# Attention scores of a pair's first three units as four 64 by 64 products each, with the masked block written by ScalarE in advance

## The chip, the core and the metric

The program runs on one core of a Trainium2 chip. The core has five engines with queues of their own: TensorE (PE, matrix products, with the loading of its weights listed apart as PEld), VectorE (DVE), ScalarE (ACT), GpSimd (POOL) and SyncE (SP, which issues most transfers). The metric is the time of one execution in microseconds; of several runs the median counts. Lower is better.

## What is computed

Block-causal attention over 4 batches of 8 heads (576 positions, 64 channels per head, blocks of 64), then two mixture-of-experts layers on the 2304 tokens. The change touches the attention alone:

```python
scores = scale * np.matmul(q, k.transpose(0, 1, 3, 2))
pos = np.arange(S)                                   # S = 576
mask = pos[:, None] // 64 >= pos[None, :] // 64      # blocks of 64
scores = np.where(mask, scores, -1000000000.0)
scores = scores - np.max(scores, axis=-1, keepdims=True)
attn = np.exp(scores)
attn = attn / (np.sum(attn, axis=-1, keepdims=True) + 1e-09)
return np.matmul(attn, v)
```

Behind it `_moe_ref` sends each token to one of 8 experts, or past them, and `_moe2_ref` to two of 8.

## The kernel before

Two heads of one batch make a pair, with their channels on partitions 0 to 63 and 64 to 127; there are 16 pairs, n = 0 to 15, four for each batch. A pair has four units of query rows. Unit 0 holds query tiles 0 and 1 (128 rows each), unit 1 tile 2, unit 2 tile 3, and unit 3 the last 64 rows of both heads. Tile t needs the keys up to position 128(t + 1), so it has 128, 256, 384 or 512 columns of scores. In the last 128 of these, the upper 64 rows must not see the last 64 columns: that corner is the masked block.

The loop from line 957 takes one unit in each turn i and staggers the work. Turn i issues the score products of unit i (`scores`), its row maxima (`highest`), a transposition of the next pair's keys or queries on VectorE (`turned`, in a pair's first two turns, line 542), the transposes of unit i - 2 on TensorE and their copies out of PSUM (`tr`), three steps of the products with V of unit i - 4 (`av`), what stands in `mid`, the exponentials of unit i on ScalarE (`soft`), the rest of `av`, and what stands in `fill`. Each engine runs its instructions strictly in the order in which this loop writes them.

PSUM holds two score buffers, `seta` and `setb`, that units use in turn, the sums of `av` and two single banks, 4 and 5. The two banks are handed out in turn to whoever asks (`bank`, line 72): the transposes of `tr`, those of the finished rows (`turned_rows`, line 693), the router products of a batch (`side_logits`, line 712; in `mid` of the second turn of pairs 5, 9 and 13, and again at the end), and the prefix sums of the routing (`prefix`, lines 187 to 191, two for each batch). A bank is free for the next writer when its copy out is done.

Which of ScalarE and VectorE makes such a copy is decided by `evac` (line 501) when the program is written: it keeps a running sum of planned time for both engines, `load`, that `spend` adds to, and gives the copy to the engine whose sum would be lower. The routing steps are not in these sums. A copy on ScalarE is line 508, one on VectorE line 511.

`scores` (line 549) issues for each tile and each head one product with 64 rows of the array and all its 128 columns; the two heads take the two halves of the rows. `highest` (line 568) first adds -1e9 to the masked block on VectorE (line 575), then takes the maxima (line 578) and scales them (line 585).

Of the kernel before, what the change touches and what calls it, by code (L numbers as in the profile page):

```python
# [8 lines left out]
F32 = mybir.dt.float32  # L9
# [4 lines left out]
AF = mybir.ActivationFunctionType  # L14
OP = mybir.AluOpType
# [4 lines left out]
P = 128  # L20
# [27 lines left out]
def moe_kernel(ctx, tc, q, k, v, w_skip, w_gate, w1, w2, w_gate2, w_noise, noise, w1b, w2b, out):  # L48
    nc = tc.nc
    B, H, S, HD = q.shape  # L50
# [292 lines left out]
    def run(steps):  # L343
        for _ in steps:
            pass
# [135 lines left out]
    with ExitStack() as actx:  # L481
        pa = actx.enter_context(tc.tile_pool(name="pa", bufs=1, space=PSUM))
# [3 lines left out]
        ac = actx.enter_context(tc.tile_pool(name="ac", bufs=1))  # L486
# [8 lines left out]
        def spend(engine, ns):  # L495

            load[engine] += ns
            for e in load:
                load[e] = max(load[e], load[engine] - 2000)
# [36 lines left out]
        SCALE = HD ** -0.5  # L536
# [9 lines left out]
        LAST = 3  # L546
        sets = [0]

        def scores(U):


            kt, qt = flat[U.n]
            U.S = pa.tile([P, 2, 512], F32, name="set" + "ab"[sets[0] % 2])
            sets[0] += 1
            rows = [slice(64 * h, 64 * h + 64) for h in range(2)]
            if U.u < LAST:
                for c, t in U.tiles:
                    for h in range(2):
                        nc.tensor.matmul(U.S[:, h, c:c + (t + 1) * P], qt[rows[h], t * P:(t + 1) * P],  # L559
                                         kt[rows[h], 0:(t + 1) * P], start=True, stop=True, skip_group_check=True)  # L560
            else:
                for w in range(2):
                    for h in range(2):
                        c = (w + h) % 2
                        nc.tensor.matmul(U.S[rows[h], c, 0:288], qt[rows[h], 512:576], kt[rows[h], 288 * c:288 * c + 288],  # L565
                                         start=True, stop=True, skip_group_check=True)

        def highest(U):


            U.negm = wk.tile([P, 4], F32, name="negm", bufs=4)
            if U.u < LAST:
                lo = U.S[0:64].rearrange("p h (a c) -> p h a c", c=64)
                lo = lo[:, :, 1:6:4] if U.u == 0 else lo[:, :, 2 * U.u + 3]
                nc.vector.tensor_scalar(lo, lo, -1e9, None, op0=OP.add)
                spend(nc.vector, 150 + 133 * len(U.tiles))
                for i, (c, t) in enumerate(U.tiles):
                    nc.vector.tensor_reduce(U.negm[:, 2 * i:2 * i + 2], U.S[:, :, c:c + (t + 1) * P], axis=AX.X,
                                            op=OP.max, negate=True)
                    spend(nc.vector, 150 + 2.08 * (t + 1) * P)  # L580
            else:
                nc.vector.tensor_reduce(U.negm[:, 0:1], U.S[:, :, 0:288], axis=AX.XY, op=OP.max, negate=True)
                spend(nc.vector, 150 + 1.04 * S)
            n = 2 * len(U.tiles) or 1
            nc.vector.tensor_scalar(U.negm[:, 0:n], U.negm[:, 0:n], SCALE, None, op0=OP.mult)
            spend(nc.vector, 100)
# [276 lines left out]
        units = []  # L863
        for n in range(NS):
            for u in range(NU):
                U = Obj()
# [53 lines left out]
        for n in range(NS):  # L920
            b, hp = divmod(n, 4)
            i = NU * n + NU - 1 + SK2
# [28 lines left out]
        def first_turned(c0, c1):  # L951
            for i in range(2):
                turned(0, i, c0, c1)

        first_turned(0, CUT)
        i = 0
        while i < len(units) + SK2 or any(j >= i for j in (*fill, *mid)):
            if i < len(units):
                U = units[i]
                n, g = U.n, U.u  # L960
                if g == 0 and n % 4 == 0:
                    new_rows(U.b)
                if g == 0 and 0 < n < NS - 2:
                    load_qk(n + 2)
                if g == 0 and 0 < n < NS - 1:
                    load_v(n + 1)
                scores(U)
                if i == 0:
                    first_turned(CUT, S)
                highest(U)  # L970
                if n == 0 and g == 1:
                    load_v(1)
                    load_qk(2)
                g0 = 1 if n == 0 else 0
                if n + 1 < NS and g0 <= g < g0 + 2:
                    turned(n + 1, g - g0)
            if 0 <= i - SK1 < len(units):
                tr(units[i - SK1])
            main = av(units[i - SK2]) if 0 <= i - SK2 < len(units) else iter(())
            for _ in range(3 if units[i - SK2].u < LAST else 2):  # L980
                next(main, None)
            for f, a in mid.get(i, []):
                f(*a)
            if i < len(units):
                soft(U)
            run(main)
            for f, a in fill.get(i, []):
                f(*a)
            i += 1
# [478 lines left out]
    with ExitStack() as cctx:  # L1468
# [14 lines left out]
        h = [hh, cp.tile([P, FC, M], F32R, name="hl")]  # L1483
# [240 lines left out]
```

## Time and profile before

| | us |
|---|---|
| median of 3 runs | 851.49 |
| lowest and highest run | 850.37, 852.3 |
| the profiled execution | 852.99 |
| span of the profiled execution | 851.1 |
| granted clock of TensorE, mean | 0.991 |

| engine | busy us | share of the span |
|---|---|---|
| TensorE | 813.9 | 96% |
| VectorE | 498.8 | 59% |
| ScalarE | 336.6 | 40% |
| GpSimd | 342.9 | 40% |

The page of the profile gives the busy time of each engine over the whole span. Its chain of work that ended last follows the end back to what released each step. For this change the stretch of the attention counts, about the first 236 us; there the chain, the waits and the timeline have to be read by themselves, because the later stages have other limits. Times of rows are in us from the span's start unless marked ns.

### The profile page before, as it was taken

Reading aid. Unit: us, or ns where it says so; the run is one execution under the profiler, and the core shown is the slowest. Engines: PE = TensorE matmul, PEld = TensorE weight load, DVE = VectorE, ACT = ScalarE, POOL = GpSimd, SP = SyncE. Lnnn points to the kernel's source line nnn. Section 1 sums busy time; section 2 is a strip of 40 time slices with the busy share of each in tenths; the row PEclk is TensorE's granted clock in tenths of the full one; section 3 lists DMA queues with packets and bytes.
Section 4 is the critical chain, followed back from the end, with each engine's and each line's share of the span. In section 5 each row is a group of like instructions: output and inputs, shape, how many; then the busy total and the mean of one; then the engine's idle time right before and its main releaser. Section 6 shows DMA issues by size and latency. Waiting matters only on the chain.

```text
span 851.1 us, 16018 instructions
## 1 busy us (share of the span) xinstructions
PE 813.9 (96%) x5916; PEld 711.0 (84%) x5916; DVE 498.8 (59%) x1470; ACT 336.6 (40%) x608; POOL 342.9 (40%) x286
## 2 busy tenths in 40 slices
PE   6999999999999999999999999999999999999994
PEld 3777777777787768777889999989999899999993
DVE  5777978879543544537747466355562655635631
ACT  4676655565422322313417335324252253423410
POOL 1043220120442315433436048365383572833745
PEclk9999999999999999999999999999999999999997
DMA  7777646662028887987728256355464564541314
GB/s 122 164 143 185 141 119 148 88 125 61 18 72 262 300 276 235 289 205 287 229 47 239 86 140 148 78 144 116 136 127 84 141 140 119 117 77 13 43 16 45
DMA packets 157063, 117.56 MB, mean 138 GB/s; under 512 B 109688, under 2 KB 123760, under 8 KB 156976
## 3 DMA queue, kind: packets, MB, share of 16 engines
q1 hardware_dynamic: 133696, 92.00, 39.5%
q0 software_dynamic: 20848, 24.15, 16.4%
q8 instruction: 48, 0.79, 0.4%
q10 hardware_dynamic: 2432, 0.30, 0.2%
q14 instruction: 39, 0.32, 0.2%
HBM read 95.89 MB, written 22.82 MB: 139 GB/s over the span
## 4 chain that ended last, share of the span: by engine, by line
PE 82%; DVE 6%; DMA 6%; issue 1%; another core or an unknown queue 1%; ACT 1%; SPq 1%; POOL 0%; POOLq 0%; DVEq 0%; ACTq 0%
PE bank L414 23%; PE sums L641 7%; PE bank L1198 5%; PE bank L613 4%; PE bank L1521 4%; PE bank L1523 4%; PE bank L1522 4%; PE bank L457 4%; PE bank L459 4%; PE bank L458 4%; PE seta L559 3%; PE bank L398 2%; PE setb L565 2%; DMA st<-in_moe_w_dram 2%; PE sums L659 2%
## 5 line engine op out<-in xcount | busy, mean ns | idle before, releaser
L1531 POOL DMA_INDIRECT out_dram<-y,toq x77 | 150.4, 1954 | 94.2 <-DVE y L1530 75.0
L414 PE MATMUL bank<-xh,w1h 128*128 128x296 f32 (+2 forms) x512 | 122.0, 299 | 0.8 <-ACT xh L401 0.8
L414 PE MATMUL bank<-xl,w1h 128*128 128x296 f32 (+2 forms) x512 | 120.8, 297 | 0.6 <-DVE xl L402 0.4
L414 PE MATMUL bank<-xh,w1l 128*128 128x296 f32 (+2 forms) x512 | 120.6, 297 | 0.0
L417 ACT ACTIVATE hh<-bank 128x296 fp32r<-128x296 f32 (+2 forms) x128 | 47.5, 412 | 147.7 <-PE bank L414 144.6
L418 DVE SCALAR_TENSOR_TENSOR hl<-bank,hh 128x296 fp32r<-128x296 f32 (+2 forms) x128 | 54.0, 458 | 77.9 <-ACT hh L417 72.5
L414 PEld LDWEIGHTS bank<-xh,w1h 128*128 128x128 f32 x512 | 87.1, 189 | 1.7 <-ACT xh L401 0.9
L414 PEld LDWEIGHTS bank<-xl,w1h 128*128 128x128 f32 x512 | 86.9, 189 | 1.1 <-DVE xl L402 1.1
L414 PEld LDWEIGHTS bank<-xh,w1l 128*128 128x128 f32 x512 | 86.4, 188 | 0.0
L155 ACT ACTIVATE q2h<-st 128x1024 fp32r<-128x1024 f32 x28 | 57.7, 2062 | 61.4 <-PE bank L459 61.4
L641 PE MATMUL sums<-v,ptS 128*128 128x65 f32 x640 | 80.1, 271 | 0.3 <-issue 0.2
L641 PEld LDWEIGHTS sums<-v,ptS 128*128 128x128 f32 x640 | 77.0, 192 | 1.3 <-issue 0.9
L1521 PE MATMUL bank<-hh,q2h 128*128 128x336 f32 x224 | 72.7, 325 | 0.0
L1523 PE MATMUL bank<-hh,q2l 128*128 128x336 f32 x224 | 71.1, 318 | 0.0
L1522 PE MATMUL bank<-hl,q2h 128*128 128x336 f32 x224 | 71.0, 317 | 0.0
L214 POOL DMA_INDIRECT rows<-xd,t3x x35 | 36.2, 1035 | 83.8 <-PE bank L398 76.4
L508 ACT ACTIVATE ptS<-bank 128x384 f32<-128x384 f32 (+2 forms) x97 | 48.1, 524 | 52.0 <-PE bank L613 44.3
L206 POOL DMA_INDIRECT lists<-ent,seats x26 | 25.6, 986 | 104.3 <-DVE seats L844 100.2
L164 DVE TENSOR_TENSOR q2l<-st,q2h 128x1024 fp32r<-128x1024 f32 x28 | 56.3, 2012 | 14.4 <-ACT q2h L155 14.4
L613 PEld LDWEIGHTS bank<-idf,P 128*128 128x128 f32 x320 | 35.0, 144 | 31.3 <-ACT P L595 11.4
L457 PE MATMUL bank<-q2h,hh 128*128 128x512 f32 x136 | 53.8, 396 | 0.0
L458 PE MATMUL bank<-q2l,hh 128*128 128x512 f32 x136 | 53.5, 394 | 0.0
(389 smaller groups left out, 1656.3 us busy)
## 6 DMA issues: line engine op xcount, KB each, us to landing
st<-in_moe_w_dram SPq DMA_DIRECT2D x98, 512.0 KB
r<-in_moe_w_dram SPq DMA_DIRECT2D x32, 512.0 KB
out_dram<-zero SPq DMA_DIRECT2D x19, 256.0 KB
kraw<-in_k_dram SPq DMA_DIRECT2D x60, 72.0 KB
qraw<-in_q_dram SPq DMA_DIRECT2D x60, 72.0 KB
v<-in_v_dram SPq DMA_DIRECT2D x32, 128.0 KB
xd<-Xe SPq DMA_DIRECT2D x2, 1040.0 KB
out_dram<-y,toq POOLq DMA_INDIRECT x77
```

The source lines that it names most:

```text
L155: nc.scalar.activation(h, src, AF.Copy)
L164: on_low.tensor_sub(l, src, h.bitcast(F32))
L414: nc.tensor.matmul(s[i][:, :c1 - c0], a, part[:, c, c0:c1], start=st, stop=sp)
L418: nc.vector.scalar_tensor_tensor(b, r, 0.0, a.bitcast(F32), op0=OP.max, op1=OP.subtract)
L457: nc.tensor.matmul(o[:n], a, wh, start=f == 0, stop=False)
L458: nc.tensor.matmul(o[:n], a, wl, start=False, stop=False)
L613: nc.tensor.transpose(pt[:, c:c + P], U.P[:, h, c:c + P], idf)
L641: nc.tensor.matmul(o[:, h, t, :], U.T[h][:, c + j * P:c + (j + 1) * P], vb[:, j, h, :], start=j == 0, stop=j == t)
L1521: nc.tensor.matmul(o[:, :n], wh, a, start=f == 0, stop=False)
L1522: nc.tensor.matmul(o[:, :n], wh, b, start=False, stop=False)
L1523: nc.tensor.matmul(o[:, :n], wl, a, start=False, stop=f == FC - 1)
L1531: st = nc.gpsimd.indirect_dma_start(out=out.rearrange("n (a d) -> (n a) d", d=P), in_=y, in_offset=None, compute_op=OP.add, out_offset=bas ...
```

## The change

Four things change. The two products of a tile become four: each head's is cut into the upper and lower 64 query rows, g = 0 and 1, that take the left and the right half of the array's columns; the upper half computes 64 columns less, so the masked block is not computed. A new function, `masked_set`, allocates the score buffer two units ahead and lets ScalarE write the constant into the masked block, one copy of 64 x 128 elements for each tile; it stands right behind the exponentials of the unit that used the buffer before. The addition of line 575 goes. And the planned times follow: 300 ns more for ScalarE for each written block, and 283 ns (one tile) or 416 ns (two) less for VectorE for each unit.

```diff
+        hidden = ac.tile([64, 1], F32, name="hidden")
+        nc.vector.memset(hidden, -1e9 / SCALE)
+        masked = []
+
+        def masked_set(U):
+            S = pa.tile([P, 2, 512], F32, name="set" + "ab"[sets[0] % 2])
+            sets[0] += 1
+            if U.u < LAST:
+                for c, t in U.tiles:
+                    lo = S[0:64, :, c + t * P + 64:c + t * P + P]
+                    nc.scalar.activation(lo, hidden[:, :, None].to_broadcast([64, 2, 64]), AF.Copy)
+                    spend(nc.scalar, 300)
+            return S
+
         def scores(U):
             kt, qt = flat[U.n]
-            U.S = pa.tile([P, 2, 512], F32, name="set" + "ab"[sets[0] % 2])
-            sets[0] += 1
+            U.S = masked.pop(0)
             rows = [slice(64 * h, 64 * h + 64) for h in range(2)]
             if U.u < LAST:
                 for c, t in U.tiles:
-                    for h in range(2):
-                        nc.tensor.matmul(U.S[:, h, c:c + (t + 1) * P], qt[rows[h], t * P:(t + 1) * P],
-                                         kt[rows[h], 0:(t + 1) * P], start=True, stop=True, skip_group_check=True)
+                    for g in range(2):
+                        n = t * P + 64 * (g + 1)
+                        for h in range(2):
+                            nc.tensor.matmul(U.S[rows[g], h, c:c + n], qt[rows[h], t * P + 64 * g:t * P + 64 * g + 64],
+                                             kt[rows[h], 0:n], start=True, stop=True, skip_group_check=True)
...
             if U.u < LAST:
-                lo = U.S[0:64].rearrange("p h (a c) -> p h a c", c=64)
-                lo = lo[:, :, 1:6:4] if U.u == 0 else lo[:, :, 2 * U.u + 3]
-                nc.vector.tensor_scalar(lo, lo, -1e9, None, op0=OP.add)
-                spend(nc.vector, 150 + 133 * len(U.tiles))
...
+        masked.extend(masked_set(U) for U in units[:2])
         first_turned(0, CUT)
...
             if i < len(units):
                 soft(U)
+            if i + 2 < len(units):
+                masked.append(masked_set(units[i + 2]))
             run(main)
```

The planner's sums thereby give 48 of its 156 copies to another engine: 34 that were ScalarE's become VectorE's (18 of 128x384 elements, 11 of 128x512), 14 the other way (9 of 64x128). Two places show what that does to the order. Names with numbers are single buffers; `ptS` is the copy of a unit's transposes, `ptS2` its short last piece, `negm` the maxima.

The first place is the second turn of pair 9, on VectorE, from the transposition of the keys on, before:

```order
L542 STREAM_TRANSPOSE kt_1814<-kraw_1610 128x576
L575 TENSOR_SCALAR setb_1854<-setb_1854 64x2x64
L578 TENSOR_REDUCE negm_1857<-setb_1854 128x2
L585 TENSOR_SCALAR negm_1857<-negm_1857 128x2
L542 STREAM_TRANSPOSE qt_1815<-qraw_1611 128x576
L511 COPY ptS2_1870<-bank5_1869 64x128
```

and now:

```order
L542 STREAM_TRANSPOSE kt_1904<-kraw_1689 128x576
L591 TENSOR_REDUCE negm_1950<-setb_1863 128x2
L598 TENSOR_SCALAR negm_1950<-negm_1950 128x2
L542 STREAM_TRANSPOSE qt_1905<-qraw_1690 128x576
L511 COPY ptS_1955<-bank4_1954 128x512
```

The addition is gone, and the copy of the wide transposes out of bank 4 is now the last of these, in the place of the short one out of bank 5. On TensorE the router products take bank 4 right behind it, before:

```order
L559 MATMUL setb_1854<-kt_1633,qt_1634 128x384 x2
L621 MATMUL bank4_1862<-idf_73,P3_1775 128x128 x4
L625 MATMUL bank5_1869<-idf_73,P3_1775 64x128
L641 MATMUL sums_330<-v2_154,ptS_1760 128x65 x3
L712 MATMUL bank4_1876<-xt0_1246,wcat_95 32x128 x4
```

and now (line 712 is line 725 there):

```order
L576 MATMUL setb_1863<-kt_1714,qt_1715 64x320 x2
L576 MATMUL setb_1863<-kt_1714,qt_1715 64x384 x2
L634 MATMUL bank4_1954<-idf_73,P3_1861 128x128 x4
L638 MATMUL bank5_1961<-idf_73,P3_1861 64x128
L654 MATMUL sums_348<-v2_154,ptS_1846 128x65 x3
L725 MATMUL bank4_1968<-xt0_1309,wcat_95 32x128 x4
```

The two score products became four; the order behind them is the same, so the router products now follow a bank that VectorE empties. Pairs 5 and 13 read alike at this place.

The second place is the third turn of pair 10, on VectorE, before:

```order
L542 STREAM_TRANSPOSE qt_2061<-qraw_1792 128x576
L818 TENSOR_TENSOR OH_2146<-e8_80,atb_2099 128x80
L820 TENSOR_TENSOR ohb_2147<-OH_2146 128x40
L821 COPY ent2_2148<-tokc_97 128x10
L575 TENSOR_SCALAR seta_2152<-seta_2152 64x2x64
L578 TENSOR_REDUCE negm_2155<-seta_2152 128x2
L585 TENSOR_SCALAR negm_2155<-negm_2155 128x2
L511 COPY ptS_2166<-bank5_2165 128x384
```

and now:

```order
L542 STREAM_TRANSPOSE qt_2160<-qraw_1880 128x576
L511 COPY ptS2_2234<-bank5_2233 64x128
L831 TENSOR_TENSOR OH_2248<-e8_80,atb_2200 128x80
L833 TENSOR_TENSOR ohb_2249<-OH_2248 128x40
L834 COPY ent2_2250<-tokc_97 128x10
L591 TENSOR_REDUCE negm_2258<-seta_2191 128x2
L598 TENSOR_SCALAR negm_2258<-negm_2258 128x2
L511 COPY ptS_2262<-bank4_2261 128x384
```

VectorE's copy behind the maxima was that of bank 5 and is now that of bank 4. Bank 4 is the one that the second prefix sum (line 187) of that batch takes next, before as now.

## Rows read from the trace of the kernel before

**Rows 1.** Page, first part: busy time, share of the span, instructions.
```profile
PE 813.9 (96%) x5916; PEld 711.0 (84%) x5916; DVE 498.8 (59%) x1470; ACT 336.6 (40%) x608; POOL 342.9 (40%) x286
```

**Rows 2.** Stretches: length, busy us (instructions) of PE, PEld, DVE, ACT, POOL; clock, DMA.
```profile
15.00:65.00 50.00, 50.00 (x428) 38.77 (x424) 38.70 (x88) 34.22 (x68) 11.20 (x16) 1.00 0.81 151
65.00:155.00 90.00, 86.09 (x795) 66.10 (x793) 75.03 (x287) 53.42 (x115) 19.20 (x24) 0.99 0.63 144
```

**Rows 3.** Chain of work, pair 2: start, us, engine, output, line, instructions.
```profile
29.69 0.86 PE seta L559 x8
...
33.24 0.85 PE setb L559 x4
...
36.07 1.06 PE seta L559 x4
37.13 0.81 PE bank L613 x6
37.94 1.73 PE sums L641 x16
39.67 1.12 PE setb L565 x8
...
42.47 0.86 PE seta L559 x8
```

**Rows 4.** Lines 559 and 565: weight loads, ns min/median/max, starts, shapes.
```profile
L559 PEld LDWEIGHTS seta<-kt,qt x192: 182/186/330, 5.3 to 218.6; 64*128 64x128 f32 x192
...
L565 PEld LDWEIGHTS setb<-kt,qt x128: 129/133/228, 14.6 to 224.1; 64*64 64x64 f32 x128
```

**Rows 5.** Timeline, second turn of pair 9: start, us, engine, line, operation [idle before].
```profile
128.47 0.92 PE L559 MATMUL setb<-kt,qt 64*128 64x384 f32 x4
...
129.51 0.29 DVE L575 TENSOR_SCALAR setb<-setb 64x128 f32<-64x128 f32 x1 [1.06 <-PE setb L559]
...
129.83 0.96 DVE L578 TENSOR_REDUCE negm<-setb 128x2 f32<-128x768 f32 x1
...
130.07 0.60 ACT L508 ACTIVATE ptS<-bank 128x512 f32<-128x512 f32 x1 [0.21 <-PE bank L621]
130.72 1.08 PE L712 MATMUL bank<-xt,wcat 128*32 128x128 f32 x32
...
131.70 0.24 DVE L511 COPY ptS<-bank 64x128 f32<-64x128 f32 x1
```

**Rows 6.** Groups of the attention by shape: count, busy us, mean ns, idle before.
```profile
L575 DVE TENSOR_SCALAR seta<-seta 64x256 f32<-64x256 f32 x16 | 6.7, 421 | 1.1 <-PE seta L559 0.8
...
L508 ACT ACTIVATE ptS<-bank 64x128 f32<-64x128 f32 x6 | 1.6, 262 | 3.1 <-PE seta L559 3.1
...
L511 DVE COPY ptS<-bank 128x512 f32<-128x512 f32 x1 | 0.7, 683 | 0.0
```

**Rows 7.** Waits of TensorE from 15 to 225: total us, times, longest.
```profile
PE bank L613 <- DVE ptS L511: 3.4, 3, 1.4
...
PE bank L712 <- ACT ptS L508: 0.6, 1, 0.6
```

**Rows 8.** Timeline, up to the third turn of pair 10.
```profile
143.44 0.42 DVE L575 TENSOR_SCALAR seta<-seta 64x256 f32<-64x256 f32 x1
...
150.73 0.18 PE L187 MATMUL bank<-ohb,tri 128*128 128x40 bf16 x1 [1.00 <-DVE seta L575]
...
150.76 1.22 DVE L578 TENSOR_REDUCE negm<-seta 128x2 f32<-128x1024 f32 x1
...
152.10 0.55 DVE L511 COPY ptS<-bank 128x384 f32<-128x384 f32 x1
```

**Rows 9.** The 3.3 us behind it: a stretch as in Rows 2, and its chain.
```profile
152.60:155.90 3.30, 3.30 (x22) 1.95 (x20) 3.16 (x19) 1.78 (x4) 0.00 (x0) 0.50 0.48 78
...
152.19 1.74 PE setb L565 x8
153.93 1.47 PE bank L613 x6
```

## The prediction

> **What bounds the kernel now.** I read the page's busy shares first, then stretches, then the chain of waits inside the attention. TensorE is busy 96% of the span, no other engine over 59% [rows 1]. The stretches show the same where the change sits: from 15 to 65 us TensorE has no idle time, VectorE is busy 38.7 of the 50 us and ScalarE 34.2; from 65 to 155, where the routing of finished batches is mixed in, TensorE is idle 3.9 of 90 us [rows 2]. The chain of pair 2 says it step by step: from 29.69 to 42.47 all is TensorE, 12.78 us for a pair [rows 3]. So in the attention an edit is worth what it does to TensorE's own products and waits; what it takes from VectorE is worth something only at the places where TensorE waits for VectorE. The later stages begin when the attention ends, and TensorE bounds most of them, so I let a shift of the attention's end come through in full.
>
> The profiled execution took 852.99 us, 1.5 above the median of the runs, 851.49. I make the sum as a difference and add it to either.
>
> **The score products.** What one unit takes: 512 columns 1.06 us, 384 columns 0.85 us [rows 3]. 128 columns more cost 0.21 us, so 512 columns cost 0.84 and some 0.21 us is a fixed part at the unit's start. For 384 columns it is the same: 0.63 + 0.22. The last unit already has products of 64 by 64: 1.12 us for 8 instructions of 288 columns [rows 3]. Two heads run side by side, so four follow one another: 4 x 288 x 1.64 ns = 0.94 (at 2 cycles a column, 0.96), and the fixed part is 0.16 to 0.18. That fits the weight loads: 186 ns with 128 columns of the array, 133 ns with 64 [rows 4]; the difference, 53 ns, is the 0.05 us.
>
> If the two halves of the array's columns run side by side as the two halves of its rows do now, a tile still takes the time of its longer half, which has as many columns as before. The masked block saves no time then; only the shorter weight load is saved, 0.05 us a unit. For unit 0 there is a second effect: it now stands behind products of a quarter of the array and changes the form of product. Within one form no gap shows at all: 16 products with V take 1.73 us, 0.108 each [rows 3]. So of its 0.21 us I take another 0.10 (bounds 0 and 0.16) away, since four-quarter products would follow four-quarter products. A pair: 3 x 0.05 + 0.10 = 0.25 us (bounds 0.10 and 0.31). Eleven of the 16 pairs are bound by TensorE throughout; the first, where TensorE waits for loads, gives 0.1, and four are treated below with their waits. **Minus 2.7 - 0.1 = minus 2.8 us** (bounds minus 1.2 and minus 3.5).
>
> That quarters with the same rows can run together is the one thing that this rests on. The row that bears on it: 32 router products of 128 columns take 1.08 us [rows 5]. They have the same 128 rows and differ in their 32 columns of the array. By the slope above each takes 0.21 us alone over two instructions, 0.105 for one; one after another 32 would take 3.4 us. 1.08 us is eight groups of four and a load. So column parts over one set of rows do run side by side.
>
> The Trainium skill, "TensorE: Matmul & The Clock Gate", Part 3 under "What overlaps and what doesn't", says otherwise of the loading: a weight load overlaps products in flight only when its row group differs, and the halves g = 0 and g = 1 have the same row group. By that rule the two halves would follow one another, which is rival D below. The row of the router products speaks against the rule.
>
> **The additions that go.** 48 of them. The wide one (unit 0) is 0.42 us [rows 6], the others 0.29 [rows 5]: 16 x (0.42 + 0.29 + 0.29) = 16 us of VectorE. In the stretches where VectorE is not the last to be waited for this is nothing. And the planner gives most of it back: VectorE gains 34 copies and loses 14, net 15 of 128x384 at 0.55 us [rows 8], 11 of 128x512 at 0.68 [rows 6], less nine and two short ones that it hands over and four that it takes, some 14 us.
>
> **The mask writes.** 64 blocks, two for unit 0 (4 tiles a pair). The trace has no such write; the nearest row is ScalarE's copy of 64x128 out of PSUM, 262 ns [rows 6]. It reads one value for a block, so I take 0.26 us as its price, with 0.1 to 0.4 as bounds: 17 us of ScalarE (6 to 26), while it loses copies of about 12 us or more. It stands right behind ScalarE's own exponentials of the unit that had the buffer, the next products into that buffer come a turn later, behind transposes, and ScalarE is busy 68% in the stretch [rows 2]. So I cost it at nothing. If that cover is gone, 0.26 us for a unit is at stake (rival E). Queued behind a write on ScalarE are the copies of the next transposes; they come after a turn's products, so a delay of 0.26 us has room.
>
> **The copies that change engine, at the places where TensorE waits.** Here the change adds waits.
>
> Pair 9, second turn: the router products need bank 4. Before, ScalarE copies the wide transposes out at 130.07 in 0.60 us, and the products start at 130.72, right behind it [rows 5]. Now VectorE does this, behind its maxima, their scaling and the transposition of the queries. Maxima at once when the scores are there (129.51 less 0.05, the addition being gone): 0.96 for the maxima [rows 5], 0.12 for the scaling (from the end of the maxima at 151.98 to the copy at 152.10 [rows 8]), 0.78 for the transposition [rows 8], 0.68 for the copy [rows 6]. Together 2.54, and 0.06 for the signals: 132.06 in place of 130.72. **Plus 1.34 us.** The order is the same in pairs 5 and 13. In pair 13 I take the same, **plus 1.34**. In pair 5 TensorE waited 0.6 us at this step already [rows 7], so **plus 0.75**. Bounds for each: 0, if VectorE should come to the transposition early and the products with V behind these steps were to stretch, and 1.6, if VectorE is still in the routing.
>
> Pair 10, third turn: the prefix sum starts at 150.73, having waited 1.00 us for VectorE [rows 8]. Now bank 4 is emptied by VectorE behind the maxima of that turn. These began at 150.76. Three additions ahead of them in a stretch in which VectorE does not pause go (0.42 [rows 8], and two of 0.29), a short copy of 0.24 [rows 5] comes: start at 150.00. From the start of the maxima to the copy are 1.34 us, and the copy takes 0.55 [rows 8]: the bank is free at 151.89, **1.15 us later**. Part comes back behind it, since VectorE comes to the next steps with less queued; I take 0.4 of it, which leaves **plus 0.75** (bounds 0 and 1.15).
>
> In pairs 6 and 14 TensorE waits for VectorE's copies of transposes (three waits, 3.4 us in all, the longest 1.4 [rows 7]). There a copy is 512 wide now and was 64 wide, while an addition of 0.29 goes: 0.68 - 0.24 - 0.29 = 0.15; I take plus 0.1 for each, **plus 0.2**, and no saving of products in these pairs. In pair 15, the third of these waits, the addition goes and nothing comes: **minus 0.3**.
>
> **The sum:** -2.8 + 1.34 + 1.34 + 0.75 + 0.75 + 0.2 - 0.3 = **+1.3 us**: 854.3 for the profiled execution, 852.8 against the median. What is gained 0.05 to 0.1 us at a time is lost at four waits.
>
> **The clock.** From 152.6 to 155.9, behind the wait of pair 10, the granted clock is 0.50, that is 1.2 GHz, and the last unit's products take 1.74 us for 1.12, the transposes 1.47 for 0.81 [rows 3, 9]: 0.62 + 0.66 = 1.3 us for such a stretch. Before it TensorE had stood idle. The new waits make TensorE idle for 1.3 us at places where it did not idle before; whether the clock falls there the trace of before cannot say.
>
> **The rivals.**
> A, the forecast, +1.3 us: 852.8 (851 to 854.3).
> B, faster. The waits are mostly covered (VectorE reaches the copies sooner, because the additions before them are gone as well, or TensorE would have waited later anyway) and the saving stands. Saving at 0.28 a pair, waits of 0.5 to 1 us in all: -3.2 + 0.7 = -2.5, 849; at the bounds 848. For it: no waiting of TensorE from 15 to 65 us; against it: the copy stands behind the maxima in VectorE's order, and an order does not become shorter than its 2.55 us.
> C, slower, by the clock. One to three of the new idle places are followed by a stretch at 1.2 GHz, 1.3 us each: +2.6 to +5.2, so 854 to 856.5. It decides from one such stretch on. For it: the stretch of [rows 9]; against it: the mean clock from 65 to 155 is 0.99 with several waits in it [rows 2].
> D, the four products do not do what is meant: the halves follow one another. Each tile's upper half has 64, 192, 320, 448 columns, 1024 a pair, at 1.64 ns 1.7 us; 16 pairs, 27 us: 879. Against it the router products [rows 5].
> E, a mask write comes late on ScalarE and the next scores wait: 0.26 us for every second unit beyond the first, some 24 places over half the pairs, less cover: +2 us on the forecast, 855.
>
> **How the numbers follow.** A 0.46, B 0.24, C 0.24, D 0.04, E 0.02. A measurement of this kernel can tell about 0.2% from no change, 1.7 us: faster is below 849.8, slower above 853.2. A's middle lies inside, its upper end beyond: 0.36 same, 0.10 slower. B: 0.20 faster, 0.04 same. C, D and E: slower, 0.30. Together faster 0.20, same 0.40, slower 0.40. Since cases of both signs hold much of the chance, the range goes from B's middle to C's end, 848.5 to 856.5, and leaves out D and half of B's better end; A's own range is 851 to 854.3.
>
> **What would show it.** In the profile after: three score units a pair at about 1.01, 0.80 and 0.70 to 0.76 us (D: 1.8 for the 512-column unit); weight loads of 64x64 at 133 ns; the regular pair at 12.5 us in place of 12.78; waits of TensorE at the router products of pairs 5, 9 and 13 for VectorE's copy, 1.3 us each; the prefix sum of pair 10 waiting about 2 us; VectorE's busy time little changed. Wrong if the regular pair stays at 12.8 (then the fixed part is not the weight load), if the router products follow the transposes without waiting, or if stretches at half clock are many.

## The result

The changed kernel is slower: 862.24 us in the median (859.77 to 863.11, four runs) against 851.25 us of before, a ratio of 1.0109 with an interval of 1.0077 to 1.0140. The prediction had 852.8 us with a range up to 856.5. Four of twelve later executions of one kernel of the experiments, the kernel before with three copies, lie over 1.5% above its fastest and are left out of its numbers as slow ones.

| | before | after |
|---|---|---|
| median, us | 851.25 | 862.24 |
| the profiled execution: time, span, us | 852.99, 851.1 | 859.77, 857.9 |
| its mean granted clock | 0.991 | 0.985 |
| granted clock of the other three runs | | 0.983 |

The profiled execution of after is its fastest. I split each time in two: a stretch at 1.2 GHz in which TensorE is busy takes twice as long, so span x (1 - mean clock) is about what the lower clock costs, and span x mean clock is what is left. This is an estimate; the last 10 us of every kernel stand at 1.2 GHz and add the same 5 us or so to each. Before, its profiled execution: 7.7 us by the clock and 843.4 left; after, mean of four runs: 14.2 and 845.8. So **of the 8.9 us between these two some 2.4 are lost at full clock, and 6.5 by the clock.** The medians are 11 us apart, since the profiled execution of before (852.99 us) took longer than any of its runs.

The page of after, first part, answers to [rows 1]:

```profile
PE 814.2 (95%) x6172; PEld 708.2 (83%) x6172; DVE 495.1 (58%) x1443; ACT 343.7 (40%) x652; POOL 342.5 (40%) x286
```

VectorE has 3.7 us less to do, ScalarE 7.1 more: the planner has given the relief back, as forecast. The chain of work of after from 41 to 55 us (start, us, engine, output, line), and two rows of TensorE's timeline that bound a pair, answer to [rows 3]:

```profile
42.11 0.65 PE seta L576 x10
...
45.46 0.81 PE setb L576 x8
...
48.25 1.02 PE seta L576 x8
...
51.81 1.12 PE setb L582 x8
```
```profile
41.80 0.33 PE L576 MATMUL seta<-kt,qt 64*64 64x64 f32 x2
...
54.30 0.33 PE L576 MATMUL seta<-kt,qt 64*64 64x64 f32 x2
```

The unit with 512 columns takes 1.02 us for 1.06, the one with 384 columns 0.81 for 0.85, and unit 0 starts among the last products of the unit ahead. A pair takes 54.30 - 41.80 = 12.50 us in place of 12.78. The saving is 0.28 us where 0.25 was forecast.

Its waits of TensorE from 15 to 235 us (total, times, longest), to be held against [rows 7]:

```profile
PE bank L626 <- DVE ptS L511: 5.9, 5, 2.6
PE bank L725 <- DVE ptS L511: 4.2, 3, 1.4
PE bank L187 <- DVE ptS L511: 1.9, 2, 1.2
```

The three waits at the router products are there, 1.38 to 1.39 us each. The timeline of the second turn of pair 9 (start, us, engine, line, operation, idle before) answers to [rows 5]; behind it TensorE's timeline goes on, and the last fence has two stretches as in [rows 2], the one behind this wait, and one in pair 15:

```profile
128.79 0.96 DVE L591 TENSOR_REDUCE negm<-setb 128x2 f32<-128x768 f32 x1 [1.27 <-PE setb L576]
...
129.79 0.17 DVE L598 TENSOR_SCALAR negm<-negm 128x2 f32<-128x2 f32 x1
...
129.97 0.78 DVE L542 STREAM_TRANSPOSE qt<-qraw 128x576 f32<-128x576 f32 x1
130.67 0.65 DVE L511 COPY ptS<-bank 128x512 f32<-128x512 f32 x1
...
131.38 1.08 PE L725 MATMUL bank<-xt,wcat 128*32 128x128 f32 x32 [1.39 <-DVE ptS L511]
```
```profile
135.52 1.99 PE L576 MATMUL seta<-kt,qt 64*64 64x448 f32 x8
...
138.76 2.27 PE L654 MATMUL sums<-v,ptS 128*128 128x65 f32 x16
```
```profile
15.00:65.00 50.00, 50.00 (x496) 37.82 (x494) 38.48 (x84) 36.79 (x80) 11.14 (x16) 1.00 0.78 152
65.00:155.00 90.00, 82.62 (x854) 62.43 (x851) 70.75 (x257) 53.57 (x128) 19.16 (x24) 0.96 0.62 141
132.70:139.50 6.80, 6.80 (x32) 4.96 (x32) 3.52 (x22) 2.37 (x7) 0.00 (x0) 0.50 0.75 171
228.20:235.20 7.00, 7.00 (x35) 5.21 (x33) 3.46 (x10) 2.12 (x4) 1.73 (x2) 0.51 0.04 3
```

The wait is as long as the prediction said, to 0.05 us. What it did not have is the 6.8 us at 1.2 GHz (0.50) right behind: there the unit with 512 columns takes 1.99 us instead of 1.09.

Where the time comes from is seen in the starts of the score units, after less before. They are 1.18 us ahead when pair 5 begins. Pair 5's router products cost 0.75. From the second to the last unit of pair 9 they fall back by 4.48 us: 1.38 the wait, 3.1 the half clock. Pair 10 costs 0.85 net of a half-clock stretch that before has there too, pair 13 1.32, pair 15 2.70. The last unit starts 7.98 us late (231.58 for 223.60). What is left of these sums, -2.1 us, is the products' saving less smaller waits, such as those for the routing steps on VectorE (1.3 us in three places, 0.7 in before).

Pair 10 (timeline of after, answers to [rows 8]):

```profile
152.94 0.24 DVE L511 COPY ptS<-bank 64x128 f32<-64x128 f32 x1
...
153.24 0.55 PE L626 MATMUL bank<-idf,P 128*128 128x128 f32 x3 [0.72 <-DVE ptS L511]
...
154.98 0.55 DVE L511 COPY ptS<-bank 128x384 f32<-128x384 f32 x1
...
155.59 0.18 PE L187 MATMUL bank<-ohb,tri 128*128 128x40 bf16 x1 [1.18 <-DVE ptS L511]
```

There are two waits. The short copy of bank 5, which I had only counted as 0.24 us in VectorE's order, is itself waited for: the transposes of the second head need that bank, and the copy stands behind the transposition of the queries. And in pair 15 (timeline of after):

```profile
225.68 0.96 DVE L591 TENSOR_REDUCE negm<-setb 128x2 f32<-128x768 f32 x1 [4.75 <-PE seta L576]
...
227.49 0.88 PE L626 MATMUL bank<-idf,P 128*128 128x128 f32 x6 [2.62 <-DVE ptS L511]
```

TensorE waits 2.62 us where before it waited 1.4, the longest of [rows 7], and from 228.2 on it stands at 1.2 GHz; the 2.70 us of pair 15 are both together.

### The profile page after: what moved, and what is told of

The parts are those of the page before. It is cut to its first block, busy times and chain, and to the rows that moved or that the text cites. A ratio compares the mean times of both kernels' runs of the same rounds, so it can differ in the third digit from the quotient of the medians.

```text
span 857.9 us, 16496 instructions
## 1 busy us (share of the span) xinstructions
PE 814.2 (95%) x6172; PEld 708.2 (83%) x6172; DVE 495.1 (58%) x1443; ACT 343.7 (40%) x652; POOL 342.5 (40%) x286
## 4 chain that ended last, share of the span: by engine, by line
PE 79%; DVE 8%; DMA 7%; issue 2%; SPq 1%; POOL 1%; ACT 1%; POOLq 0%; DVEq 0%; ACTq 0%
PE bank L414 23%; PE sums L654 7%; PE bank L1537 4%; PE bank L1539 4%; PE bank L1538 4%; PE bank L1214 4%; PE bank L626 4%; PE bank L457 3%; PE bank L458 3%; PE bank L459 3%; PE seta L576 3%; PE setb L582 2%; PE bank L398 2%; DMA st<-in_moe_w_dram 2%; PE bank L1228 2%
## 5 line engine op out<-in xcount | busy, mean ns | idle before, releaser
L654 PE MATMUL sums<-v,ptS 128*128 128x65 f32 x640 | 82.9, 277 | 0.5 <-DVE Xo L683 0.2
L654 PEld LDWEIGHTS sums<-v,ptS 128*128 128x128 f32 x640 | 79.9, 198 | 1.6 <-issue 0.9
L164 DVE TENSOR_TENSOR q2l<-st,q2h 128x1024 fp32r<-128x1024 f32 x28 | 56.4, 2014 | 14.2 <-ACT q2h L155 14.2
L626 PE MATMUL bank<-idf,P 128*128 128x128 f32 x320 | 49.1, 292 | 7.5 <-DVE ptS L511 5.9
L508 ACT ACTIVATE ptS<-bank 128x512 f32<-128x512 f32 (+2 forms) x76 | 36.7, 499 | 47.1 <-PE bank L626 42.9
```

The costliest lines, as they stand in the source:

```text
L164: on_low.tensor_sub(l, src, h.bitcast(F32))
L626: nc.tensor.transpose(pt[:, c:c + P], U.P[:, h, c:c + P], idf)
L654: nc.tensor.matmul(o[:, h, t, :], U.T[h][:, c + j * P:c + (j + 1) * P], vb[:, j, h, :], start=j == 0, stop=j == t)
```

## The experiments

**Theory 1**: the loss comes from the copies that moved to VectorE. TensorE waits for them, and standing idle brings the clock down behind some of these waits. **Rival 2**: the clock falls by the new products themselves, that use all four quarters of the array, or the mask writes cost time; the moved copies cost only their waits. Medians of before differ between the groups of runs (848.9 to 857.6 us), so each kernel is held against before of its own group. "Clock" is span x (1 - mean clock), "rest" is span x mean clock, means over the runs; for before itself "clock" is 7.6 to 11.0 us, from group to group.

| kernel | median us | ratio to before (interval) | clock us | rest us |
|---|---|---|---|---|
| before, first group | 856.58 | | 10.9 | 844.0 |
| changed, old copies | 852.62 | 0.9959 (0.9929 to 0.9990) | 8.3 | 842.1 |
| changed, three copies back | 856.17 | 0.9988 (0.9956 to 1.0020) | 9.0 | 845.3 |
| before, new copies | 877.05 | 1.0247 (1.0183 to 1.0311) | 24.7 | 850.7 |
| before, three copies | 870.37 | 1.0174 (1.0105 to 1.0243) | 19.8 | 848.1 |
| before, second group | 857.58 | | 11.0 | 844.7 |
| products alone | 855.41 | 0.9967 (0.9935 to 0.9998) | 12.6 | 841.4 |
| changed, waits filled | 860.09 | 1.0023 (0.9995 to 1.0052) | 11.4 | 846.7 |
| before, one copy | 862.04 | 1.0073 (1.0038 to 1.0108) | 13.7 | 847.9 |
| changed | 861.86 | 1.0038 (1.0011 to 1.0065) | 11.7 | 847.4 |
| before, third group | 852.57 | | 8.8 | 842.2 |
| before, three copies, filled | 855.98 | 1.0047 (1.0025 to 1.0069) | 8.0 | 846.8 |
| before, three copies | 860.94 | 1.0095 (1.0058 to 1.0133) | 14.2 | 845.1 |
| changed, old copies | 852.62 | 1.0003 (0.9983 to 1.0023) | 11.1 | 839.6 |
| products alone | 853.76 | 1.0013 (0.9993 to 1.0032) | 10.2 | 841.7 |
| before, fourth group | 853.37 | | 8.9 | 841.9 |
| changed | 859.81 | 1.0088 (1.0056 to 1.0119) | 13.1 | 845.8 |
| changed | 861.38 | 1.0104 (1.0076 to 1.0132) | 13.2 | 846.3 |
| changed, waits filled | 859.45 | 1.0087 (1.0057 to 1.0117) | 13.6 | 844.5 |
| changed, waits filled | 859.46 | 1.0082 (1.0050 to 1.0115) | 12.6 | 844.6 |
| before, fifth group | 848.88 | | 7.6 | 839.3 |
| changed, pair 10's copies back | 848.58 | 1.0008 (0.9989 to 1.0028) | 6.9 | 840.7 |
| changed, pair 10's and the three back | 846.62 | 0.9972 (0.9955 to 0.9989) | 7.3 | 837.5 |

### The copies, all and three

In all kernels that fix the copies, `evac` reads the engine of each of the 156 copies from a string instead of asking the planner:

```diff
-            if load[nc.scalar] + a <= load[nc.vector] + v:
+            made[0] += 1
+            if COPIES[made[0]] == "A":
```

The changed kernel with the string of before:

> The changed kernel with every copy out of the two banks on the engine that it had before the change; only the assignment of the 156 copies is undone. Theory 1 (the loss comes from the copies that moved to VectorE: TensorE waits for them, and behind some of these waits it runs at 1.2 GHz): no wait at the router products of pairs 9 and 13, no stretch at 1.2 GHz behind pair 9, the regular pair stays at 12.5 us, and the time is 3 to 4.5 us below before, about 847.5. Rival 2 (products on all four quarters of the array themselves bring the clock down, or the mask writes cost time): stretches at 1.2 GHz are as long as in the changed kernel, and the time stays above before, 853 to 857.

The changed kernel with its own string, but "A" for the wide transposes ahead of the router products of pairs 5, 9 and 13 (numbers from 1):

```diff
-COPIES[43], COPIES[84], COPIES[121] = "D", "D", "D"
+COPIES[43], COPIES[84], COPIES[121] = "A", "A", "A"
```

> The changed kernel with three of its copies given back to ScalarE: those of the wide transposes out of bank 4 ahead of the router products in the second turn of pairs 5, 9 and 13. Theory 1: the waits there go (0.75 + 1.38 + 1.32 = 3.4 us) and with them the stretch at 1.2 GHz from 132 to 140 us (some 3 us): 855 to 856; the wait of pair 10 and that of pair 15 stay with what follows them. Rival 2 (the clock falls by the products): only the waits go, the stretch stays: 858.5 to 859.

The kernel before with the changed kernel's string, and with its own string but those three "D":

```diff
-COPIES[43], COPIES[84], COPIES[121] = "A", "A", "A"
+COPIES[43], COPIES[84], COPIES[121] = "D", "D", "D"
```

> The kernel before with every copy out of the two banks on the engine that it has in the changed kernel; the products and the additions on VectorE are as before. Theory 1: the waits at the router products of pairs 5, 9 and 13 come, each 0.3 us longer than in the changed kernel since the addition is still ahead of the maxima, and stretches at 1.2 GHz with them: 860 to 865. Rival 2: the waits alone, 4 to 6 us, with no more half clock than before: 855 to 857.

> The kernel before with three copies given to VectorE, those of the wide transposes ahead of the router products in pairs 5, 9 and 13; nothing else. Theory 1: three waits of about 1.0, 1.65 and 1.65 us, and a stretch at 1.2 GHz behind pair 9 of some 3 us: 857 to 859. Rival 2: the waits alone: 855 to 856, with the granted clock at full level from 130 to 150 us.

Measured: the old copies give a kernel 0.4% below before, and its trace has no stretch at 1.2 GHz in the attention. The waits of theory 1 came as expected, but their price is far above it: the three copies alone, without any of the new products, make the kernel before 13.8 us slower, where theory 1 had 6 to 8 and the waits themselves are 4.5 (5.1 for the 0.6 of before). All copies make it 20 us slower. Of the 13.8, 8.9 are clock. The waits of before with three copies from 15 to 235 us, and the 10 us behind the waits of pairs 9 and 13 in the same trace:

```profile
PE bank L716 <- DVE ptS L515: 5.1, 3, 1.7
...
PE bank L187 <- DVE seta L579: 1.0, 1, 1.0
```
```profile
133.88:143.88 10.00, 10.00 (x89) 7.20 (x91) 5.25 (x31) 3.82 (x10) 0.00 (x0) 0.83 0.75 155
194.31:204.31 10.00, 10.00 (x100) 7.63 (x100) 5.84 (x29) 3.27 (x9) 0.00 (x0) 0.83 0.43 107
```

A clock of 0.83 over 10 us is 3.4 us at 1.2 GHz in each. Rival 2 falls as the main cause: the old products lose as much, or more, when they wait. A small share of the new products in the clock is not excluded: alone, further down, they lose 1.6 and 1.4 us more by it than before does, and the changed kernel with old copies 2.6 less in this group but 2.3 more in the third.

### One copy, the products alone, and the waits filled

The kernel before with one "D", for the wide transposes ahead of the router products of pair 9:

```diff
-COPIES[84] = "A"
+COPIES[84] = "D"
```

> The kernel before with a single copy given to VectorE, that of the wide transposes ahead of the router products in pair 9. By theory 1 one wait of 1.7 us (1.38 and the addition of 0.33) and a stretch at 1.2 GHz behind it that costs some 3 us: 4 to 6 us above before. By rival 2 the wait alone: 1.5 to 2 us above before.

Measured: +4.5 us in the median. TensorE's timeline at the place, and the stretch behind it:

```profile
133.14 1.71 PE L716 MATMUL bank<-xt,wcat 128*32 128x128 f32 x32 [1.71 <-DVE ptS L515]
```
```profile
133.40:147.00 13.60, 13.60 (x81) 10.08 (x71) 4.83 (x29) 3.62 (x9) 0.00 (x0) 0.50 0.56 115
```

One wait of 1.71 us is followed by 13.6 us at 1.2 GHz in this execution, which costs 6.8; over ten runs the clock costs 2.7 us more than in before. So a price for a wait, if there is one, exists only as a mean over executions.

The products alone, in the kernel before, with masked block, additions and copies as they were:

```diff
-                    for h in range(2):
-                        nc.tensor.matmul(U.S[:, h, c:c + (t + 1) * P], qt[rows[h], t * P:(t + 1) * P],
-                                         kt[rows[h], 0:(t + 1) * P], start=True, stop=True, skip_group_check=True)
+                    for g in range(2):
+                        for h in range(2):
+                            nc.tensor.matmul(U.S[rows[g], h, c:c + (t + 1) * P],
+                                             qt[rows[h], t * P + 64 * g:t * P + 64 * g + 64],
+                                             kt[rows[h], 0:(t + 1) * P], start=True, stop=True, skip_group_check=True)
```

> The kernel before with one part of the change: four products of 64 by 64 parts for a tile, all of them over the tile's full columns. The masked block is computed, the additions on VectorE stay, and every copy stays on its engine. If the saving comes from the shorter weight load and from unit 0 staying with one form of product, a pair takes 12.5 us as in the changed kernel, and the time is 3 to 4.5 us below before. If it comes from the masked block that is not computed, a pair stays at 12.78 us and the time at that of before.

TensorE's timeline of the products alone:

```profile
41.28 0.33 PE L564 MATMUL seta<-kt,qt 64*64 64x128 f32 x2
...
47.66 1.09 PE L564 MATMUL seta<-kt,qt 64*64 64x512 f32 x8
...
53.78 0.33 PE L564 MATMUL seta<-kt,qt 64*64 64x128 f32 x2
```

A pair takes 53.78 - 41.28 = 12.50 us, as in the changed kernel. So the masked block that is not computed saves TensorE nothing; the products' form does all of it. The whole kernel gains 3.3 us of rest, and 0.3% of time in this group.

Now the changed kernel with useless products in its three waits. They go into columns of the next unit's buffer that its own products overwrite:

```diff
             for f, a in mid.get(i, []):
+                if f is side_logits and i < len(units):
+                    kt, qt = flat[U.n]
+                    for _ in range(2):
+                        for h in range(2):
+                            r = slice(64 * h, 64 * h + 64)
+                            nc.tensor.matmul(masked[0][:, h, 0:384], qt[r, 0:P], kt[r, 0:384], start=True, stop=True,
+                                             skip_group_check=True)
                 f(*a)
```

> The changed kernel with idle work in the place of its three waits at the router products (second turn of pairs 5, 9, 13): four score products of 384 columns, about 1.3 us, are issued right ahead of the router products into columns of the next unit's score buffer that its own products then overwrite. Nothing that counts is computed less or earlier. Theory 1 (TensorE standing idle lets the clock fall): the three waits shrink to 0 to 0.3 us, the products take their place, so the waits give nothing back, but the stretch at 1.2 GHz behind pair 9 goes: 2 to 6 us below the changed kernel on the same chip. Rival 2 (the clock falls by what the products draw): no gain or a loss of up to 1 us, and the stretch stays or grows.

> The changed kernel once more, so that it and the other three have runs on one chip: 9 to 12 us above before, with waits of 1.38 us at the router products of pairs 5, 9 and 13 and one or more stretches at 1.2 GHz between 130 and 160 us.

Filled and unfilled differ by 1.8 us in the median, and only 0.3 us of the means is clock. And the changed kernel itself is here only 0.4% above before: before loses more to its clock on this chip (11.0 us) than where the case was first measured (7.7), the changed kernel less (11.7 for 14.2). Inconclusive, so the same filling went into the kernel before with three copies, where the waits and the loss are larger (480 columns, about 1.9 us, a buffer taken for it):

> The kernel before with three copies given to VectorE (the waits of 1.71 us at the router products of pairs 5, 9 and 13), and idle work in the place of these waits: four score products of 480 columns, about 1.8 us, right ahead of the router products, into columns of the next unit's score buffer that its own products overwrite. Theory 1 (standing idle at these places lets the clock fall behind them): no stretch at 1.2 GHz within 10 us behind the three places, and though TensorE has the same 5 us less for useful work, the time is 5 us or more below that of the same kernel without the filling. Rival 2 (standing idle has nothing to do with it): the same time as without the filling or up to 1 us more, with as much time at 1.2 GHz.

> The kernel before with three copies given to VectorE, once more, beside the filled one on the same chip: 9 to 14 us above before, of which the waits are 4.3 us, the rest stretches at 1.2 GHz.

TensorE's timeline of the filled kernel in pair 9, and its two stretches from 65 to 225 us:

```profile
132.11 1.88 PE L993 MATMUL seta<-kt,qt 64*128 64x480 f32 x8
133.93 1.08 PE L716 MATMUL bank<-xt,wcat 128*32 128x128 f32 x32
```
```profile
65.00:155.00 90.00, 86.68 (x798) 65.81 (x797) 73.53 (x272) 51.32 (x110) 19.22 (x24) 1.00 0.61 140
155.00:225.00 70.00, 66.97 (x600) 50.03 (x599) 55.92 (x205) 39.21 (x87) 15.65 (x16) 1.00 0.41 82
```

The wait is gone, the router products start at 133.93, within 0.1 us of where they start unfilled in the first group's trace (133.88) and in this group's (133.92), as they do in pairs 5 and 13 of this group, and the kernel is **5.0 us faster for doing useless work** (855.98 for 860.94; by the means 4.6, give or take 3.5; theory 1 asked for 5 or more, so this is at its edge). All of it is clock: 8.0 against 14.2 us. In the kernel before this decides for theory 1: it is the idle time that is paid for, beyond its own length. A single trace can't show it: the unfilled kernel's trace of this group has the three waits of 1.71 us and no stretch at 1.2 GHz behind any. Its median is 8.4 us above before here, in the first group it was 13.8.

> The changed kernel with the copies as before, once more, beside the products alone: 3 to 5 us below before on the same chip. If the mask writes by ScalarE and the additions that go are worth nothing here, within 1 us of the products alone; if VectorE's relief counts at the waits of pairs 6, 10, 14 and 15, 1 to 3 us below it.

> Four products of 64 by 64 parts for a tile, all over the full columns, additions and copies as before, once more: 2 to 4 us below before on the same chip; the regular pair 12.5 us.

In this third group neither is faster than before: the old copies gain 2.7 us of rest and give back 2.2 by the clock, the products alone 0.5 and 1.4. So the gain of 0.3 to 0.4% of the first two groups is not firm. The trace of the old copies has two stretches at 1.2 GHz this time, at 216 to 223 us behind a wait of 2.65 us in pair 15 and at 237 to 240. Additions and mask writes together (the first kernel less the second) come to 2.1 us of rest here; the planner's times play no part, since both strings are fixed.

### Which waits of the changed kernel count

> The changed kernel, beside its filled form on the same chip. 4 to 11 us above before, of which about 2.5 are at full clock and the rest time at 1.2 GHz.

> The changed kernel with idle score products in the place of its three waits at the router products, once more. Theory 1 (idle time of 1.38 us lets the clock fall as that of 1.71 us does): 2 us or more below the changed kernel, all of it less time at 1.2 GHz. If waits of this length do not count: within 1 us of it.

> As the changed kernel three places ahead; the two together give 24 executions.

> As the filled kernel ahead; the two together give 24 executions.

Measured: the filled form is 1.5 us of rest better and loses as much to the clock, 13.1 us in the mean against 13.2. Theory 1 had 2 us or more, all of it clock: for waits of this length in this kernel that did not come. In the traces the filling does what it should: with the four traces of filled kernels, 12 filled places, no stretch at 1.2 GHz begins within 5 us behind one; of 25 unfilled ones with waits of 1.38 or 1.71 us, nine have one (four of 15 of 1.38 us, five of ten of 1.71). But in the changed kernel other stretches stay: behind pair 10 at 152 to 154 us in all three filled traces, and at 225 to 228 in pair 15. Over all traces with the two waits of pair 10, 0.72 and 1.18 us, filled or not, six of eight have such a stretch at or behind them. So the three waits are not the main place. The last two runs gave the four copies around pair 10 back (the last one of pair 9 and three of pair 10), without and with the three:

```diff
-COPIES[95], COPIES[96], COPIES[97], COPIES[98] = "D", "D", "A", "D"
+COPIES[95], COPIES[96], COPIES[97], COPIES[98] = "A", "A", "D", "A"
```

> The changed kernel with the four copies around the third turn of pair 10 (the last of pair 9 and the first three of pair 10) on the engines that they had before; the three copies ahead of the router products stay on VectorE. If the prefix sum's place carries the rest of the loss: its waits of 0.73 and 1.18 us and the stretch at 1.2 GHz at 150 to 160 us go, and the kernel stands 4 to 7 us above before in place of 8. If not: 7 to 8 us above before, with as much time at 1.2 GHz.

> The same with the three copies ahead of the router products on ScalarE as well, so that the waits of pairs 5, 9, 10 and 13 are as before: at most 1 us above before, more likely 1 to 3 us below, with the waits of pairs 6, 14 and 15 left as they are in the changed kernel.

Measured: with pair 10's copies back the kernel is at before's time, 1.0008, against 1.0088 and 1.0104 of the changed kernel in the group ahead (it has no runs in this one); 4 to 7 us above before were expected. With the three as well it is faster than before by 0.28% (0.11 to 0.45); that is one group, and a gain of 0.4% of the first group did not come again in the third. The router products' waits of the kernel with pair 10's copies back, 15 to 225 us, and its two stretches:

```profile
PE bank L729 <- DVE ptS L515: 4.1, 3, 1.4
```
```profile
65.00:155.00 90.00, 83.63 (x917) 63.64 (x917) 73.63 (x274) 55.93 (x133) 19.17 (x24) 1.00 0.63 144
155.00:225.00 70.00, 66.30 (x686) 50.50 (x686) 55.46 (x192) 43.35 (x101) 17.59 (x18) 1.00 0.40 77
```

The three waits of 1.38 us are all there and the clock stands at 1.00. Giving the three copies back as well is worth 3.1 us of rest and nothing by the clock (7.3 for 6.9): here these waits cost what they take, 4.1 us less the 1.0 that stays at pair 5, and no more. The waits of that last kernel from 15 to 225 us, and two stretches:

```profile
PE bank L630 <- DVE ptS L515: 2.4, 2, 1.2
PE bank L630 <- DVE sla L811: 1.3, 3, 0.5
PE bank L729 <- ACT ptS L512: 1.0, 1, 1.0
PE bank L187 <- DVE ptS L515: 0.8, 1, 0.8
```
```profile
65.00:155.00 90.00, 85.23 (x931) 64.64 (x927) 74.21 (x278) 58.31 (x139) 19.18 (x24) 1.00 0.64 145
155.00:225.00 70.00, 67.87 (x700) 52.21 (x701) 55.35 (x192) 43.56 (x103) 17.68 (x19) 1.00 0.39 77
```

The prefix sum's wait of 1.18 us and the one ahead of it are gone, and from 65 to 225 us the clock stands at 1.00. The long wait of pair 15 is gone too, in the one trace of each, though its copies are those of the changed kernel.

Two things stay open. With the three copies back and pair 10's waits left, the kernel was already at before's time (0.9988) with 9.0 us of clock against before's 10.9, while filling the same three waits left it at 1.0085: what a wait costs seems to depend on what else stands near it, and the two gifts don't add. And the wait of pair 15 has two sizes in the same kernel (the changed one: 2.62, 1.32, 2.59, 2.58 us): VectorE and ScalarE both stand there for some us while GpSimd issues six scatters, in before too (3.15 us). The moved copies are not its cause: with the old copies it is 0.90 in one trace and 2.65 in another, and in before with one copy 2.94. What is, and why it is absent in the last two kernels, no run tells.

## Why the prediction was wrong

- **The bound and the products: right.** 12.50 us a pair, 0.28 us saved where 0.25 was taken; 1.02, 0.81 us for units where 1.01 and 0.80 were said. (In the working for the last unit, 0.94 us is 4 x 288 x 0.82 ns, the slope of one instruction; the 1.64 ns printed there is that of two.) Column halves over the same rows run together, in the changed kernel and in the products alone. The rule of the Trainium skill, "TensorE: Matmul & The Clock Gate", Part 3, "What overlaps and what doesn't", that a weight load overlaps products in flight only where the row group differs, does not hold for these 64 by 64 parts: as the prediction reads it, the 512-column unit would take 1.8 us, and it takes 1.02.
- **The mask writes: right.** The loads and writes of the changed kernel by line (ns min/median/max, first and last start, shapes):

```profile
L576 PEld LDWEIGHTS seta<-kt,qt x384: 129/133/228, 5.9 to 223.8; 64*64 64x64 f32 x192
...
L561 ACT ACTIVATE seta<-hidden x48: 273/273/274, 5.3 to 222.2; 64x128 f32<-64x128 f32 x48
```

  A write takes 273 ns where 262 was taken, and the load is 133 ns, as [rows 4] had it for such parts.
- **The router products: right.** 1.38 us in pairs 9 and 13 (forecast 1.34), 0.75 more in pair 5 (forecast 0.75). Right too are pairs 6 and 14: waits of 1.18 us for 1.00 (forecast 0.1 more).
- **Pair 10: the size right, the waits not.** The forecast lengthened one wait, that of the prefix sum, by 1.15 us, and let 0.4 come back: +0.75. The starts give +0.85. The prefix sum comes 4.63 us behind the score products ahead of it (155.59 less 150.96), in before 3.55 (150.73 less 147.18): 1.08 more. But there are two waits, 0.72 + 1.18 us, where before has one of 1.00. The short copy that moved to VectorE was priced as 0.24 us in VectorE's order, but its bank is what TensorE asks for next. That the size came out nevertheless is luck in part: VectorE works without a pause from 151.08 to the end of the copy at 155.53, so the prefix sum starts then, whatever TensorE waits for ahead of it. Every moved copy has two sides, the queue that it lengthens and the bank that it holds; I looked at the second only for the wide ones.
- **Pair 15: mis-sized.** Forecast -0.3; measured between -0.1 and +1.2, by a wait whose size changes from one execution to the next and that is as long with the old copies.
- **The sum at full clock** was +1.3 us by the forecast and is +2.4 to +4.4 by the rests of the three groups in which the changed kernel ran. That alone would have left the time in the range.
- **The clock: the step that failed.** The sum of the forecast puts it at nothing. It stood in a rival, C, with a chance of 0.24, at 1.3 us for each of one to three stretches. The price was taken from the single stretch of before [rows 9], and its length with it; even there it is too low, since 3.3 us at half the clock cost 1.6. The stretches of the changed kernel's first trace are 6.8, 3.4 and 7.0 us long, and the one behind pair 9 cost 3.1; in the mean the clock takes 6.5 us more than in before (4.2 and 0.7 in two other groups). C has the mechanism and only the price wrong; the sign "if stretches at half clock are many" came true. The row that spoke against C, the mean clock of 0.99 with several waits in it [rows 2], could not carry that: the waits of before in that stretch are 0.6 to 1.0 us, those that the change makes are 1.2 to 1.4, or two close together, and the one stretch of [rows 9] stands behind one of 1.00. That length alone decides is not shown: with pair 10's copies back three waits of 1.38 us had no stretch behind them.
- **Rivals B, D, E**: the waits were not covered (B); the halves run together (D); no wait in the regular pairs is for a mask write (E). At the start of pair 1 four later traces name one, 0.2 to 1.1 us, but pair 1 starts within 0.2 us of before (17.08 to 17.42 for 17.22).

## What to carry to other kernels

Where TensorE is the bound, a wait can cost more than its own length, because of what the clock does behind it: in the kernel before 4.5 us of new waits cost 8 to 14 us. It need not: three waits of 1.38 us cost 3.1 us in the changed kernel once pair 10's were gone. So look at what an edit's planner moves: relief of an engine that nobody waits for is worth little or nothing, and 48 copies that changed queue cost more than the edit gained. Before trusting a load balancer's sums, list the few copies whose bank the bounding engine asks for next, and pin these.

## What was not expected of the hardware

Idle work in three waits of 1.71 us makes the kernel 5.0 us faster without starting the router products any earlier; the changed kernel's waits of 1.38 us show no such gain by the clock. The same program has stretches at 1.2 GHz at other places from execution to execution: behind one and the same wait of 1.71 us there were 13.6 us of them, 3.4, or none. And a store of a constant by ScalarE into 64 x 128 elements of PSUM takes 0.27 us, no less than a copy out of it.
